# A tile of its own for each PSUM bank of the Strassen chains, and another order for the first two column groups

## Chip, cores and metric

The kernel runs on one core of a Trainium2 chip. The metric is the device time of one execution in microseconds, the median of several runs. Engines are called by the profile's names: PE is TensorE (PEld its weight loads), DVE VectorE, ACT ScalarE, POOL GpSimd, SP the DMA queue of SyncE.

## What is computed

A linear attention with decay (batch 2, 8 heads, 768 steps, head size 64) gives x with 1536 tokens of 512 features. A first mixture of experts sends each token to one of 8 experts. A second one runs all tokens through 4 experts:

```python
p = domain_probs / (domain_probs.sum(-1, keepdims=True) + 1e-09)
for e in range(E):                       # E = 4, w1[e]: 512 x 1024, w2[e]: 1024 x 512
    h = np.maximum(x @ w1[e], 0.0)
    out += p[:, e:e + 1] * (h @ w2[e])
```

The change concerns this second mixture. In the profile it runs from 240.75 us to the end.

## The kernel before

Everything is float32, written as a high and a low part (`float32r`): a value is cast on ACT to its high part, and DVE subtracts that from the value to get the low part. A product of two such operands is three matmuls (high by high, high by low, low by high; `PASS`). The order of the work is written out by hand: each engine executes its instructions in the order in which the program names them, and waits are put in where tiles ask for it.

The second mixture works in 32 **column groups** n. Group n belongs to a half s of the tokens (768 each), an expert e and a quarter q of the 1024 hidden columns. Its first layer multiplies the half's features, a 2 x 2 arrangement of blocks (256 features x 384 tokens each), with a 2 x 2 arrangement of weight blocks, by seven products instead of eight (Strassen). `front(n)` (line 972) issues the seven: `product(n, i, bank, first)` is six matmuls of 384 columns, two halves of the 256 features by three passes. The token operands `X1` to `X7` are blocks of x or sums of blocks (`x_sum`, `x_hi`, `x_lo`, lines 750 to 773), made once for each half of the tokens; the weight operands are the loaded blocks `p` or sums of them `t` (`combine_w`, line 134, three instructions), each split into two parts (`split_w`, line 116).

The products gather in two PSUM banks, a and b. Bank a takes products 1, 6, 7 and 4, one on top of the other; b takes 2, and then, newly begun, 5 and 3. Between them ACT copies the state of a to a `c` tile (`kept`, line 963) and DVE adds b to it (`joined`, line 968), so the four results c11, c22, c12 and c21 come out (c21 straight from a). Each result goes through ReLU on ACT (its high part) and one DVE instruction (its low part), `evac_h`, line 955; the pair is a tile `g` of 384 tokens.

`back(n, t)` (line 1050) is the second layer of a group for the 128 tokens of tile t, t = 0 to 5: six matmuls of 512 columns into an output bank o, which gathers over the four quarters q of an expert. Behind the fourth, `leave` (line 1091) lets DVE scale the bank by the token's weight and add it to the sum in SBUF; in the last expert `send` stores it from POOL.

The main loop interleaves front(n) with the six steps of the group before: products 1, 2, step 0, product 6, step 1, products 5, 7, steps 2, 3, products 3, 4, steps 4, 5. The splits of the next weights stand in between, and `combine_w(n + 2)` on POOL at the end. `load_w` issues the weight loads of 512 KB on SP, four of them in flight.

PSUM has eight banks. The pool `ps1` gives them out as four tiles of two banks, and `twin` (line 937) hands these on: a and b are the two halves of one tile (`ab`), and the output banks of steps 0 and 1, 2 and 3, 4 and 5 share a tile each:

```python
def front(n):
    ab = twin(0, f"ab{n}")
    a, b = ab[:, 0], ab[:, 1]
...
    bk = gb[t // 2][:, t % 2]
```

The first two groups have no group before them to be interleaved with. `first_pair` (line 998) runs products of both in turn: 1, 7, 2, 6, 5, 4, 3. There products 7 and 4 have a third tile `dd`, so DVE adds dd to c12 for c22 and for c21. Meanwhile the X tiles are made; x_sum(0,3), combine_w(2) and combine_w(3) run on POOL. Six output steps of group 0 follow.

Of the kernel before, what the change touches and what calls it, by code (L numbers as in the profile page):

```python
# [54 lines left out]
def tile_retention_moe_moe(ctx: ExitStack, tc, qkv, cst, gqt, a1, a2, b1, b2, out, cap):  # L55
# [674 lines left out]
    offsets()  # L730
    xe[2] = load_xe(2)
    sctx.close()
    ps[0] = ctx.enter_context(tc.tile_pool(name="ps1", bufs=1, space=PSUM))
    nduo = [0]

    def duo(name):
# [123 lines left out]
    for e in range(E1):  # L860
# [92 lines left out]
    hq = {}  # L953

    def evac_h(n, c, src):
        h2 = hq[n, c] = ph.tile([P, 2, HT], F32R, tag="h", name=f"g{n}_{c}")
        nc.scalar.activation(out=h2[:, 0], in_=src, func=AF.Relu)  # L957
        nc.vector.scalar_tensor_tensor(  # L958
            out=h2[:, 1], in0=src, scalar=0.0, in1=h2[:, 0].bitcast(F32), op0=ALU.max,
            op1=ALU.subtract,  # L960
        )

    def kept(n, c, bk):
# [6 lines left out]
        evac_h(n, c, t)  # L970

    def front(n):
        ab = twin(0, f"ab{n}")
        a, b = ab[:, 0], ab[:, 1]
        product(n, 1, a, True)
        c11 = kept(n, "c11", a)
        yield
        product(n, 2, b, True)
        joined(n, "c11", b, c11)
        yield  # L980
        product(n, 6, a, False)
# [12 lines left out]
        evac_h(n, "c21", a[:, 0:HT])
        del ws["p", n], ws["t", n]
        yield

    def first_pair():
        add = ALU.add
        ab = [twin(n, f"ab{n}") for n in range(2)]  # L1000
        dd = twin(2, "dd")
        c11, c12, c22 = [0, 0], [0, 0], [0, 0]

        def each(i, bank, first):
            for n in range(2):
                product(n, i, dd[:, n] if bank == 2 else ab[n][:, bank], first)

        each(1, 0, True)
        c11[0] = kept(0, "c11", ab[0][:, 0])
# [12 lines left out]
        each(2, 1, True)
        x_hi(0, 4)
        for n in range(2):
            joined(n, "c11", ab[n][:, 1], c11[n])
        x_lo(0, 4)
        each(6, 0, False)
        x_hi(0, 3)
        x_lo(0, 3)
        for n in range(2):  # L1030
            c12[n] = kept(n, "c12", ab[n][:, 0])
            c22[n] = pk.tile([P, HT], F32, tag="c22", name=f"c22_{n}")
            nc.vector.tensor_tensor(out=c22[n], in0=dd[:, n, 0:HT], in1=c12[n], op=add)
        each(5, 1, True)
        for n in range(2):
            joined(n, "c22", ab[n][:, 1], c22[n])
        each(4, 2, False)
        split_w(units.index(("w", 0)))
        for n in range(2):
            c21 = pk.tile([P, HT], F32, tag="c11", name=f"c21_{n}")  # L1040
            nc.vector.tensor_tensor(out=c21, in0=dd[:, n, 0:HT], in1=c12[n], op=add)
            evac_h(n, "c21", c21)
        each(3, 1, False)
        for n in range(2):
            joined(n, "c12", ab[n][:, 1], c12[n])
            del ws["p", n], ws["t", n]

    gb = {}

    def back(n, t):  # L1050
        s, e, q = n // 16, n // 4 % E2, n % 4
        if q == 0 and t // 2 not in gb:
            gb[t // 2] = twin(3 - t // 2, f"o{n}_{t}")
        bk = gb[t // 2][:, t % 2]
        hs = [hq[n, c] for c in (("c11", "c12") if t < 3 else ("c21", "c22"))]
        cols = slice(t % 3 * P, t % 3 * P + P)
        w = ws["w", n].rearrange("p s (k d) -> p s k d", k=2)
        for k in range(2):
            for m, (sh, sw) in enumerate(PASS):
                nc.tensor.matmul(  # L1060
                    out=bk, lhsT=hs[k][:, sh, cols], rhs=w[:, sw, k],
                    start=(q == 0 and k == 0 and m == 0), stop=(k == 1 and m == 2),
                    skip_group_check=True,
                )
        if q == 3:
            leave(s, e, t, bk)
            if t % 2:
                del gb[t // 2]
            if s and e == E2 - 1:
                send(s, t)  # L1070

# [188 lines left out]
```

## Time and profile before

| | us |
|---|---|
| median of three runs | 874.26 (872.3 to 874.83) |
| profiled execution | 876.1 |
| its span, from the first to the last instruction | 874.0 |
| PE busy | 770.9 (88% of the span) |
| DVE busy | 487.0 (56%) |
| ACT busy | 339.8 (39%) |
| POOL busy | 173.8 (20%) |
| PE busy from 75 to 235 (first mixture) | 159.19 of 160 |
| PE busy from 338 to 556 (second mixture) | 191.13 of 218 |

The profile follows one execution. Where an engine was idle in front of an instruction, the row names in brackets for how long and what released it ("0.62 <-ACT c L965": for 0.62 us, until ACT's instruction that writes tile c in line 965 was done). A matmul's end is modelled; the rate of a row of matmuls is read from the start of one row to the start of the next. The granted clock of PE is given as a share of 2.4 GHz; it has two levels here, 1.00 and 0.50.

### The profile page before, as it was taken

What the parts mean: (1) busy time and instruction counts of PE and PEld (TensorE: products, weight loads), DVE (VectorE), ACT (ScalarE), POOL (GpSimd) and SP (SyncE); (2) the same over time, 40 slices, a digit from 0 to 9 for tenths busy, and PEclk for the clock granted to TensorE, in tenths of its full rate; (3) what the DMA queues carried; (4) which work ended last, traced back from release to release, by engine and by line L of the source; (5) the groups of instructions that cost most, each with busy time, mean ns of one, the idle gap of its engine ahead of it and who ended that gap; (6) DMA issues with size and microseconds to landing.
All of it is one profiled execution on the core that took longest, in us unless ns stands there. A gap on an engine that the chain in (4) does not pass through costs nothing.

```text
span 874.0 us, 11369 instructions
## 1 busy us (share of the span) xinstructions
PE 770.9 (88%) x4466; PEld 670.6 (77%) x4467; DVE 487.0 (56%) x773; ACT 339.8 (39%) x550; POOL 173.8 (20%) x165
## 2 busy tenths in 40 slices
PE   8989999999988988997998897799979979988993
PEld 6878999999976867876877776678867767877772
DVE  4888788788884453445445537543544444454431
ACT  2345666666543332332433334233423323432320
POOL 3532111321041120111111113151112111111002
PEclk9999999999998998999999998999999999999998
DMA  9966677666402211121121121022211121121001
GB/s 343 410 231 231 229 232 233 219 202 212 145 25 73 72 49 49 49 73 49 49 72 49 49 72 47 27 100 81 71 43 67 51 70 49 49 72 49 1 1 72
DMA packets 27642, 93.22 MB, mean 107 GB/s; under 512 B 3617, under 2 KB 3889, under 8 KB 27586
## 3 DMA queue, kind: packets, MB, share of 16 engines
q1 hardware_dynamic: 23042, 81.79, 27.8%
q0 software_dynamic: 2672, 7.44, 2.4%
q10 hardware_dynamic: 1872, 3.24, 1.0%
q8 instruction: 36, 0.59, 0.3%
q14 instruction: 20, 0.16, 0.1%
HBM read 86.11 MB, written 6.34 MB: 106 GB/s over the span
## 4 chain that ended last, share of the span: by engine, by line
PE 76%; DVE 13%; ACT 6%; issue 2%; DMA 1%; POOL 1%; ACTq 0%; POOLq 0%; SPq 0%; DVEq 0%
PE o L1060 28%; PE ab L948 26%; PE m L852 12%; PE m L855 6%; DVE w L127 4%; DVE c L969 3%; ACT c L965 2%; ACT w L126 2%; DVE X L772 1%; DVE x L1106 1%; ACT g_c L957 1%; DVE g_c L958 1%; PE S L248 1%; PE X L346 1%; PE O L303 1%
## 5 line engine op out<-in xcount | busy, mean ns | idle before, releaser
L1060 PE MATMUL o<-w,g_c 128*128 128x512 f32 x1152 | 299.3, 404 | 33.2 <-DVE x L1106 19.3
L948 PE MATMUL ab<-X,w 128*128 128x384 f32 x1320 | 274.2, 348 | 46.2 <-DVE c L969 27.3
L948 PEld LDWEIGHTS ab<-X,w 128*128 128x128 f32 x1320 | 237.0, 192 | 77.3 <-DVE c L969 35.2
L1060 PEld LDWEIGHTS o<-w,g_c 128*128 128x128 f32 x1152 | 218.1, 193 | 83.4 <-DVE x L1106 26.6
L127 DVE TENSOR_TENSOR w<-raw,w 128x1024 fp32r<-128x1024 f32 x128 | 157.0, 1230 | 76.7 <-ACT w L126 76.1
L126 ACT CAST w<-raw 128x1024 fp32r<-128x1024 f32 x128 | 133.4, 1048 | 1.3 <-ACT xk L365 1.2
L969 DVE TENSOR_TENSOR c<-ab,c 128x384 f32<-128x384 f32 x96 | 53.4, 556 | 140.2 <-PE ab L948 133.3
L957 ACT ACTIVATE g_c<-c 128x384 fp32r<-128x384 f32 x98 | 51.5, 525 | 198.7 <-DVE c L969 195.8
L141 POOL TENSOR_TENSOR t<-raw 128x512 f32<-128x512 f32 x30 | 39.7, 1324 | 386.2 <-DMA raw<-b 294.9
L965 ACT COPY c<-ab 128x384 f32<-128x384 f32 x94 | 45.0, 479 | 174.4 <-PE ab L948 174.4
L958 DVE SCALAR_TENSOR_TENSOR g_c<-c,g_c 128x384 fp32r<-128x384 f32 x98 | 60.9, 621 | 59.7 <-ACT g_c L957 59.7
L852 PE MATMUL m<-h,w 128*128 128x448 f32 x256 | 81.4, 377 | 0.8 <-DVE h L881 0.8
L852 PE MATMUL m<-xet,w 128*128 128x448 f32 x256 | 80.8, 375 | 1.5 <-DVE offb L549 1.5
L855 PE MATMUL m<-h,w 128*128 128x224 f32 x256 | 67.4, 263 | 0.0
L855 PE MATMUL m<-xet,w 128*128 128x224 f32 x256 | 67.4, 263 | 0.0
L852 PEld LDWEIGHTS m<-xet,w 128*128 128x128 f32 x256 | 48.0, 187 | 5.3 <-issue 1.6
L852 PEld LDWEIGHTS m<-h,w 128*128 128x128 f32 x256 | 48.0, 188 | 4.7 <-ACT w L126 1.1
L855 PEld LDWEIGHTS m<-h,w 128*128 128x128 f32 x256 | 48.8, 191 | 0.0
L855 PEld LDWEIGHTS m<-xet,w 128*128 128x128 f32 x256 | 48.8, 190 | 0.0
L1106 DVE SCALAR_TENSOR_TENSOR x<-o,tl,x 128x512 f32<-128x512 f32 x34 | 25.4, 747 | 26.1 <-PE o L1060 26.1
L127 DVE TENSOR_TENSOR w<-t,w 128x1024 fp32r<-128x1024 f32 x32 | 39.5, 1235 | 0.0
L126 ACT CAST w<-t 128x1024 fp32r<-128x1024 f32 x32 | 33.6, 1050 | 0.0
(137 smaller groups left out, 557.8 us busy)
## 6 DMA issues: line engine op xcount, KB each, us to landing
raw<-a SPq DMA_DIRECT2D x64, 512.0 KB, 4.3
raw<-b SPq DMA_DIRECT2D x64, 512.0 KB, 3.4
qk<-qkv SPq DMA_DIRECT2D x12, 512.0 KB, 7.6
kv<-qkv SPq DMA_DIRECT2D x12, 512.0 KB, 9.0
xd<-xk ACTq DMA_DIRECT2D x12, 256.0 KB, 6.4
gqs<-gqt SPq DMA_DIRECT2D x6, 256.0 KB, 7.4
iw<-cst SPq DMA_DIRECT2D x1, 272.0 KB
xe<-xd,gidx POOLq DMA_INDIRECT x16, 5.7
```

The lines of the kernel that those rows point to most:

```text
L126: nc.scalar.copy(w[:, 0], r)
L127: nc.vector.tensor_tensor(out=w[:, 1], in0=r, in1=w[:, 0].bitcast(F32), op=ALU.subtract)
L141: eng.tensor_tensor(out=c[:, 0:2], in0=b[:, 2:4], in1=b[:, 1:3], op=sub)
L852: nc.tensor.matmul(out=b2, lhsT=w[0], rhs=x, start=first, stop=last, skip_group_check=True)
L855: nc.tensor.matmul(out=b2[:, 0], lhsT=w[1], rhs=x[:, 0], start=False, stop=last, skip_group_check=True)
L948: nc.tensor.matmul(out=bk[:, 0:HT], lhsT=w[:, sw, k], rhs=x[:, sx, k], start=(first and m == 0), stop=(m == len(steps) - 1), skip_group_ch ...
L957: nc.scalar.activation(out=h2[:, 0], in_=src, func=AF.Relu)
L958: nc.vector.scalar_tensor_tensor(out=h2[:, 1], in0=src, scalar=0.0, in1=h2[:, 0].bitcast(F32), op0=ALU.max, op1=ALU.subtract,)
L965: nc.scalar.copy(t, bk[:, 0:HT])
L969: nc.vector.tensor_tensor(out=t, in0=bk[:, 0:HT], in1=t, op=ALU.add)
L1060: nc.tensor.matmul(out=bk, lhsT=hs[k][:, sh, cols], rhs=w[:, sw, k], start=(q == 0 and k == 0 and m == 0), stop=(k == 1 and m == 2), skip_ ...
L1106: nc.vector.scalar_tensor_tensor(out=to, in0=src, scalar=sc, in1=acc, op0=ALU.mult, op1=ALU.add)
```

## The change

Four things are changed.

The pool `ps1` is closed before the second mixture, and a new one, `ps2`, gives out eight tiles of one bank each (`pbank`). a and b are tiles of their own, b is a new tile when product 5 begins it again (`bb`), and each output step t has its own bank (`OB`).

`first_pair` runs the products in the order 1, 2, 5, 6, 7, 3, 4 for both groups, a and b as in `front`, with a third bank (`bb`) for 5 and 3. The tile dd is gone, and with it DVE's four sums of dd and c12.

x_sum(0,3) and combine_w(2) move from POOL to DVE, combine_w(2) to the end of `first_pair`. The sums of the two groups (`join`) stand together on DVE, ahead of the two low parts; `evac_h` is cut into its ACT half and its DVE half for that, and the g tiles are taken in the order of the groups.

Four pools get `reuse_waits="tile"`: a tile that takes the place of a closed pool's tile waits for that tile, not for the whole pool.

The diff, cut to its core:

```diff
-    ps[0] = ctx.enter_context(tc.tile_pool(name="ps1", bufs=1, space=PSUM))
+    pctx = ExitStack()
+    ps[0] = pctx.enter_context(tc.tile_pool(name="ps1", bufs=1, space=PSUM))
...
     hctx.close()
-    ph = ctx.enter_context(tc.tile_pool(name="ph2", bufs=8, side="right"))
-    pk = ctx.enter_context(tc.tile_pool(name="pk", bufs=2, side="right"))
+    pctx.close()
+    ph = ctx.enter_context(tc.tile_pool(name="ph2", bufs=8, side="right", reuse_waits="tile"))
+    pk = ctx.enter_context(tc.tile_pool(name="pk", bufs=2, side="right", reuse_waits="tile"))
+    ps2 = ctx.enter_context(tc.tile_pool(name="ps2", bufs=1, space=PSUM, reuse_waits="tile"))
...
-    def twin(k, name):
-        return ps[0].tile([P, 2, 512], F32, tag=f"duo{k}", name=name)
+    def pbank(k, name):
+        return ps2.tile([P, 512], F32, tag=f"k{k}", name=name)
...
     def front(n):
-        ab = twin(0, f"ab{n}")
-        a, b = ab[:, 0], ab[:, 1]
+        a, b = pbank(0, f"a{n}"), pbank(1, f"b{n}")
...
+        b = pbank(1, f"bb{n}")
         product(n, 5, b, True)
...
     def first_pair():
...
-        each(7, 2, True)
-        x_hi(0, 5)
-        x_lo(0, 5)
-        x_hi(0, 6)
-        x_lo(0, 6)
-        x_sum(0, 3, nc.gpsimd)
-        combine_w(2, nc.gpsimd)
-        each(2, 1, True)
...
+        each(2, b, True)
+        x_sum(0, 6, nc.vector)
+        x_hi(0, 5)
+        x_lo(0, 5)
+        each(5, bb, True)
+        x_hi(0, 6)
+        x_lo(0, 6)
+        each(6, a, False)
+        join("c11", b)
+        x_sum(0, 3, nc.vector)
...
+        each(7, a, False)
+        x_hi(0, 4)
+        x_lo(0, 4)
+        for n in two:
+            c[n, "c22"] = kept(n, "c22", a[n])
+        join("c22", bb)
+        each(3, bb, False)
...
+        each(4, a, False)
+        join("c12", bb)
...
+        combine_w(2, nc.vector)
...
     def back(n, t):
-        if q == 0 and t // 2 not in gb:
-            gb[t // 2] = twin(3 - t // 2, f"o{n}_{t}")
-        bk = gb[t // 2][:, t % 2]
+        if q == 0 and t not in gb:
+            gb[t] = pbank(OB[t], f"o{n}_{t}")
+        bk = gb[t]
```

PE in the main loop: product 4 of group 4, steps 4 and 5 of group 3 (the last quarter of an expert), products 1 and 2 of group 5. `ab` is the tile of two banks, `o0_4` the tile of steps 4 and 5, w78 a weight tile, g3 the results of group 3. Before:

```order
L948 MATMUL ab4_3675<-X0_4_3284,w76_3596 128x384 [waits DVE_49]
L948 MATMUL ab4_3675<-X0_4_3284,w76_3596 128x384 x5
L1060 MATMUL o0_4_3392<-w77_3654,g3_c21_3651 128x512 x3
L1060 MATMUL o0_4_3392<-w77_3654,g3_c22_3620 128x512 x3
L1060 MATMUL o0_4_3392<-w77_3654,g3_c21_3651 128x512 [waits DVE_49]
L1060 MATMUL o0_4_3392<-w77_3654,g3_c21_3651 128x512 x2
L1060 MATMUL o0_4_3392<-w77_3654,g3_c22_3620 128x512 x3
L948 MATMUL ab5_3798<-X0_1_3169,w78_3709 128x384 x6
L948 MATMUL ab5_3798<-X0_2_3243,w78_3709 128x384 [waits Activation_49]
```

The same place in the changed kernel, where a4, a5, b5, o0_4 and o0_5 are tiles of one bank:

```order
L951 MATMUL a4_3685<-X0_4_3334,w76_3605 128x384 [waits Activation_49]
L951 MATMUL a4_3685<-X0_4_3334,w76_3605 128x384 x5
L1091 MATMUL o0_4_3242<-w77_3664,g3_c21_3661 128x512 x3
L1091 MATMUL o0_4_3242<-w77_3664,g3_c22_3630 128x512 x3
L1091 MATMUL o0_5_3410<-w77_3664,g3_c21_3661 128x512 x3
L1091 MATMUL o0_5_3410<-w77_3664,g3_c22_3630 128x512 x3
L951 MATMUL a5_3810<-X0_1_3169,w78_3720 128x384 [waits DVE_49]
L951 MATMUL a5_3810<-X0_1_3169,w78_3720 128x384 x5
L951 MATMUL b5_3811<-X0_2_3260,w78_3720 128x384 x6
```

The matmuls and their order are the same. Product 4 waits for ACT instead of DVE, step 5 and product 2 wait for nothing, product 1 waits for DVE.

DVE in the first pair, from the first sum for c11 to the first sum for c22 out of b; c11_0 is the tile of group 0, X0_3 and X0_4 are splits of X tiles, x2 is x. Before:

```order
L969 TENSOR_TENSOR c11_0_3240<-ab0_3225,c11_0_3240 128x384
L958 SCALAR_TENSOR_TENSOR g0_c11_3287<-c11_0_3240,g0_c11_3287 128x384
L969 TENSOR_TENSOR c11_1_3245<-ab1_3226,c11_1_3245 128x384
L958 SCALAR_TENSOR_TENSOR g1_c11_3291<-c11_1_3245,g1_c11_3291 128x384
L772 TENSOR_TENSOR X0_4_3284<-x2_1152,X0_4_3284 128x768
L772 TENSOR_TENSOR X0_3_3307<-x2_1152,X0_3_3307 128x768
L1033 TENSOR_TENSOR c22_0_3312<-dd_3227,c12_0_3310 128x384
L1033 TENSOR_TENSOR c22_1_3316<-dd_3227,c12_1_3314 128x384
L969 TENSOR_TENSOR c22_0_3312<-ab0_3225,c22_0_3312 128x384
```

And in the changed kernel:

```order
L1031 TENSOR_TENSOR c11_0_3258<-ab0_1_3238,c11_0_3258 128x384
L1031 TENSOR_TENSOR c11_1_3262<-ab1_1_3240,c11_1_3262 128x384
L762 TENSOR_TENSOR x2_1152<-x2_1152 128x2x384
L971 SCALAR_TENSOR_TENSOR g0_c11_3229<-c11_0_3258,g0_c11_3229 128x384
L971 SCALAR_TENSOR_TENSOR g1_c11_3233<-c11_1_3262,g1_c11_3233 128x384
L773 TENSOR_TENSOR X0_3_3319<-x2_1152,X0_3_3319 128x768
L773 TENSOR_TENSOR X0_4_3334<-x2_1152,X0_4_3334 128x768
L1031 TENSOR_TENSOR c22_0_3337<-bb0_3243,c22_0_3337 128x384
```

The two sums for c11 stand together, x_sum(0,3) (line 762) has come in behind them, and the sums of dd are gone.

## Rows read from the trace of the kernel before

**Rows 1.** Waits of the whole run: engine, line, releaser: us, times, longest.
```profile
PE ab L948 <- DVE c L969: 27.3, 32, 5.8
PE o L1060 <- DVE x L1106: 19.3, 12, 2.0
PE ab L948 <- ACT c L965: 18.9, 30, 0.9
```

**Rows 2.** Timeline of PE in one group: start, us, instruction, count, idle before.
```profile
360.10 2.25 PE L948 MATMUL ab<-X,w 128*128 128x384 f32 x12
362.19 2.92 PE L1060 MATMUL o<-w,g_c 128*128 128x512 f32 x12
364.95 1.23 PE L948 MATMUL ab<-X,w 128*128 128x384 f32 x6
366.82 1.33 PE L948 MATMUL ab<-X,w 128*128 128x384 f32 x6 [0.65 <-DVE c L969]
...
370.75 1.22 PE L948 MATMUL ab<-X,w 128*128 128x384 f32 x6
372.60 1.33 PE L948 MATMUL ab<-X,w 128*128 128x384 f32 x6 [0.62 <-ACT c L965]
```

**Rows 3.** Timeline of ACT, then DVE, in the same stretch.
```profile
368.19 0.49 ACT L957 ACTIVATE g_c<-ab 128x384 fp32r<-128x384 f32 x1 [0.81 <-PE ab L948]
...
372.07 0.48 ACT L965 COPY c<-ab 128x384 f32<-128x384 f32 x1 [2.45 <-PE ab L948]
...
360.42 1.23 DVE L127 TENSOR_TENSOR w<-raw,w 128x1024 fp32r<-128x1024 f32 x1 [2.17 <-ACT w L126]
...
366.21 0.56 DVE L969 TENSOR_TENSOR c<-ab,c 128x384 f32<-128x384 f32 x1 [1.60 <-PE ab L948]
367.42 1.10 DVE L958 SCALAR_TENSOR_TENSOR g_c<-c,g_c 128x384 fp32r<-128x384 f32 x1 [0.65 <-ACT g_c L957]
```

**Rows 4.** Timeline of PE where an expert's last quarter leaves.
```profile
400.74 1.66 PE L1060 MATMUL o<-w,g_c 128*128 128x512 f32 x6 [1.65 <-DVE x L1106]
...
408.89 1.67 PE L1060 MATMUL o<-w,g_c 128*128 128x512 f32 x6 [2.05 <-DVE x L1106]
```

**Rows 5.** Timeline of PE in the first pair, up to group 2.
```profile
240.75 2.25 PE L948 MATMUL ab<-X,w 128*128 128x384 f32 x12
...
249.59 1.28 PE L948 MATMUL ab<-X,w 128*128 128x384 f32 x6 [2.42 <-DVE c L969]
...
266.90 9.26 PE L1060 MATMUL o<-w,g_c 128*128 128x512 f32 x30 [1.07 <-DVE c L969]
275.99 1.22 PE L948 MATMUL ab<-X,w 128*128 128x384 f32 x6
```

**Rows 6.** Timeline of DVE, then POOL, at the end of the kernel.
```profile
850.48 0.75 DVE L1106 SCALAR_TENSOR_TENSOR x<-o,tl,x 128x512 f32<-128x512 f32 x1 [1.51 <-PE o L1060]
...
851.51 0.99 POOL L1073 DMA_INDIRECT out_dram<-x,tl  x1 [62.37 <-DVE x L1106]
854.98 0.97 POOL L1073 DMA_INDIRECT out_dram<-x,tl  x1 [2.47 <-DMA out_dram<-x,tl]
```

**Rows 7.** Timeline of PE, then DVE, in group 15.
```profile
531.61 1.29 PE L948 MATMUL ab<-X,w 128*128 128x384 f32 x6
538.73 2.29 PE L948 MATMUL ab<-X,w 128*128 128x384 f32 x6 [5.82 <-DVE c L969]
...
538.13 0.54 DVE L969 TENSOR_TENSOR c<-ab,c 128x384 f32<-128x384 f32 x1
```

**Rows 8.** Timeline of ACT, then DVE, in the first pair.
```profile
242.91 0.84 ACT L768 CAST X<-x 128x768 fp32r<-128x768 f32 x1 [0.42 <-DVE x L915]
...
243.78 0.95 DVE L772 TENSOR_TENSOR X<-x,X 128x768 fp32r<-128x768 f32 x1
...
245.53 3.45 DVE L772 TENSOR_TENSOR X<-x,X 128x768 fp32r<-128x768 f32 x2
```

**Rows 9.** Busy us (instructions) of each engine in a stretch, PEclk, DMA share, GB/s.
```profile
75.00:235.00 160.00, 159.19 (x1033) 151.87 (x1032) 132.45 (x179) 102.41 (x153) 30.65 (x26) 1.00 0.68 221
```

More of the change, by code (lines that the diff above doesn't have):

```diff
@@ L899, in tile_retention_moe_moe @@
             mctx.close()
-            px2 = ctx.enter_context(tc.tile_pool(name="px2", bufs=1))
+            px2 = ctx.enter_context(tc.tile_pool(name="px2", bufs=1, reuse_waits="tile"))
         for d in range(KD):
@@ L953, in tile_retention_moe_moe, with h_tile, evac_hi, evac_lo @@
     hq = {}
-    def evac_h(n, c, src):
-        h2 = hq[n, c] = ph.tile([P, 2, HT], F32R, tag="h", name=f"g{n}_{c}")
+    gb = {}
+    OB = (7, 2, 3, 4, 5, 6)
+    def h_tile(n, c):
+        hq[n, c] = ph.tile([P, 2, HT], F32R, tag="h", name=f"g{n}_{c}")
+    def evac_hi(n, c, src):
+        if (n, c) not in hq:
+            h_tile(n, c)
+        h2 = hq[n, c]
         nc.scalar.activation(out=h2[:, 0], in_=src, func=AF.Relu)
+    def evac_lo(n, c, src):
+        h2 = hq[n, c]
         nc.vector.scalar_tensor_tensor(
@@ L961, in evac_h @@
         )
+    def evac_h(n, c, src):
+        evac_hi(n, c, src)
+        evac_lo(n, c, src)
     def kept(n, c, bk):
@@ L998, in first_pair @@
     def first_pair():
[L999 to L1009, printed above, removed]
+        two = range(2)
+        for n in two:
+            for k in ("c11", "c22", "c12", "c21"):
+                h_tile(n, k)
@@ new lines, in first_pair, with each, join @@
+        ab = [[pbank(2 * n + j, f"ab{n}_{j}") for j in two] for n in two]
+        gb.update({t: pbank(OB[t], f"o0_{t}") for t in (3, 4)})
+        bb = [pbank(6 + n, f"bb{n}") for n in two]
+        c = {}
+        def each(i, bks, first):
+            for n in two:
+                product(n, i, bks[n], first)
+        def join(k, bks):
+            for n in two:
+                nc.vector.tensor_tensor(
+                    out=c[n, k], in0=bks[n][:, 0:HT], in1=c[n, k], op=ALU.add
+                )
@@ L1010, in first_pair @@
+        a, b = [x[0] for x in ab], [x[1] for x in ab]
+        each(1, a, True)
         x_sum(0, 5, nc.vector)
+        c[0, "c11"] = kept(0, "c11", a[0])
         x_hi(0, 2)
-        c11[1] = kept(1, "c11", ab[1][:, 0])
+        c[1, "c11"] = kept(1, "c11", a[1])
         x_lo(0, 2)
+        each(2, b, True)
         x_sum(0, 6, nc.vector)
-        each(7, 2, True)
         x_hi(0, 5)
         x_lo(0, 5)
+        each(5, bb, True)
         x_hi(0, 6)
         x_lo(0, 6)
-        x_sum(0, 3, nc.gpsimd)
@@ L1021, in first_pair @@
-        combine_w(2, nc.gpsimd)
-        each(2, 1, True)
[L1023 to L1027, printed above, removed]
+        each(6, a, False)
+        join("c11", b)
+        x_sum(0, 3, nc.vector)
+        for n in two:
+            evac_hi(n, "c11", c[n, "c11"])
+        for n in two:
+            c[n, "c12"] = kept(n, "c12", a[n])
+            evac_lo(n, "c11", c[n, "c11"])
         x_hi(0, 3)
         x_lo(0, 3)
[L1030 to L1037, printed above, removed]
-        split_w(units.index(("w", 0)))
[L1039 to L1045, printed above, removed]
+        each(7, a, False)
@@ new lines, in first_pair @@
+        x_hi(0, 4)
+        x_lo(0, 4)
+        for n in two:
+            c[n, "c22"] = kept(n, "c22", a[n])
+        join("c22", bb)
+        each(3, bb, False)
+        for n in two:
+            evac_hi(n, "c22", c[n, "c22"])
+        for n in two:
+            evac_lo(n, "c22", c[n, "c22"])
+        split_w(units.index(("w", 0)))
+        each(4, a, False)
+        join("c12", bb)
+        for n in two:
+            evac_hi(n, "c21", a[n][:, 0:HT])
+            evac_hi(n, "c12", c[n, "c12"])
+            evac_lo(n, "c21", a[n][:, 0:HT])
+            evac_lo(n, "c12", c[n, "c12"])
@@ L1046, in first_pair @@
             del ws["p", n], ws["t", n]
-    gb = {}
+        combine_w(2, nc.vector)
     def back(n, t):
         s, e, q = n // 16, n // 4 % E2, n % 4
-        if q == 0 and t // 2 not in gb:
-            gb[t // 2] = twin(3 - t // 2, f"o{n}_{t}")
-        bk = gb[t // 2][:, t % 2]
+        if q == 0 and t not in gb:
+            gb[t] = pbank(OB[t], f"o{n}_{t}")
+        bk = gb[t]
         hs = [hq[n, c] for c in (("c11", "c12") if t < 3 else ("c21", "c22"))]
@@ L1065, in back @@
         if q == 3:
-            leave(s, e, t, bk)
-            if t % 2:
-                del gb[t // 2]
+            leave(s, e, t, gb.pop(t))
             if s and e == E2 - 1:
```

## The prediction

> **What bounds the kernel now.** I began with the list of waits over the whole run. TensorE is the busiest engine, and below its name three lines stand out [rows 1]: products waiting for VectorE's sums (27.3 us in 32 waits), products waiting for ScalarE's copies (18.9 us in 30), output matmuls waiting for VectorE's outgoing sums (19.3 us in 12). The counts matter more than the sums: 30 is the number of column groups from n = 2 to 31, so each of the first two waits comes once per group. Write P1 to P7 for the products of a group and b0 to b5 for its output steps.
>
> Then the timeline of one group [rows 2]. Without a wait, 12 matmuls of 384 columns take 362.19 - 360.10 = 2.09 us (1.04 a product) and 12 of 512 columns 364.95 - 362.19 = 2.76 us (1.38 a step). P3 starts at 364.95 and is through at 365.99, but P4 starts only at 366.82, named releaser VectorE's sum c. P1 starts at 370.75 and is through at 371.79, P2 starts at 372.60, named releaser ScalarE's copy c. Neither wait is for data. P4 writes the half a of the tile ab while the sum reads the half b; P2 writes b while the copy reads a. The times fit to the hundredth: the sum starts at 366.21 and lasts 0.56, the copy at 372.07 and lasts 0.48 [rows 3]. So per group 0.83 + 0.81 us are lost.
>
> Every fourth group b3 waits for the outgoing sum of b2 and b5 for that of b4, 1.65 and 2.05 us [rows 4], again two halves of one tile. The first pair of groups has true gaps (2.42 us before 249.59, 1.07 before 266.90) and, after them, the lower of TensorE's two clock levels: 30 matmuls of 512 columns take 9.26 us where 30 x 0.23 would be 6.9 [rows 5]. That is 2.4 us lost to 1.2 GHz.
>
> **The loop, n = 2 to 31.** The order of the built program shows that the four kinds of wait are gone from TensorE: P2, b1, b3, b5 wait for nobody, P4 waits for its own bank's copy alone. A group is then 7 x 1.04 + 6 x 1.38 = 15.58 us, if nothing true is late. So I lay VectorE's and ScalarE's queues along it, from P1 at 0: P2 1.04, b0 2.08, P6 3.47, b1 4.51, P5 5.90, P7 6.94, b2 and b3 7.98, P3 10.74, P4 11.78, b4 and b5 12.82, next P1 15.58. A copy starts 1.32 us after its product's start (370.75 to 372.07), a sum 1.26 us after (364.95 to 366.21) [rows 2, 3].
> - P6 needs the copy of P1: 1.32 + 0.48 = 1.80, wanted at 3.47.
> - P7 needs the copy of P6: 3.47 + 1.80 = 5.27, wanted at 6.94.
> - P3 needs the sum c22 out of its bank. The copy of P7 ends at 8.74; the two weight splits ahead on VectorE (1.23 each [rows 3], the first 1.77 ahead of b2 as at 360.42, so at 6.2) end at 8.6; the sum ends at 9.34, wanted at 10.74.
> - P1 of the next group needs the low part of c21 out of bank a. The sum c12 runs from 12.00 to 12.56, ScalarE's two activations end at 13.6 (0.5 each), VectorE's two low parts at 14.3, or 14.8 if one takes the 1.10 us of 367.42 [rows 3]. Wanted at 15.58.
> The least margin is 0.8 us. In a group with outgoing sums two of them (0.75 us each [rows 6]) stand before the sum c12 and put the last low part at 14.4 to 15.0: margin 0.6. The last two run into the next group, ahead of its first sum at 17.9, and end by 17.5. So TensorE stays the bound: 30 x 15.58 = 467.4 us. The weight loads follow the splits, which move with the groups, and are used more than a group later, so DMA costs nothing.
>
> The Trainium skill (SBUF — State Buffer, Who interferes with whom) says that a VectorE instruction with two SBUF inputs contends with a GpSimd instruction that reads SBUF. By that rule the low part of c12 takes the 1.10 us in every group that meets combine_w there, and the margin is 0.8, not 1.3: the sum stays, the first rival's chance goes up.
>
> **The exception, n = 15.** There the token half changes, and VectorE's queue has the splits of new X tiles ahead of the sum c12. P3 starts at 531.61, the sum only at 538.13, P4 at 538.73 after 5.82 us of idle [rows 7]. In the changed kernel P4, b4, b5 don't wait. Everything runs 0.9 earlier (P2's gap and the slow start behind it are gone): P3 at 530.7, b5 through at 530.7 + 2 x 1.04 + 2.76 = 535.5. P1 of n = 16 needs the low part of c21: sum at 537.2, + 0.54, two activations and a low part to 539.5. So 4.0 us of stall remain, and behind it the lower clock (P4's 2.29 us for six matmuls in that row), taken at the 2.4 us above. 6.4 us; between 4.0 and 8 without and with a longer stretch at 1.2 GHz.
>
> **The first pair.** VectorE loses the four sums that read dd (lines 1033 and 1041, about the 0.55 of another sum) and takes x_sum(0,3) and combine_w(2) from GpSimd; the rest is order. P1 of both groups runs from 240.75 to 242.83 as before. The new second step, P2, needs X2: its high part is on ScalarE from 242.91 to 243.75, its low part on VectorE from 243.78 to 244.73 [rows 8]. So a new stall of 1.0 us, where P7 filled the gap; P2 ends at 246.2. P5 and P6 need the low parts of X5 and X6. Before, these two took 3.45 us beside GpSimd, against 0.95 for one alone [rows 8]. combine_w(3) stays on GpSimd, and its buffers are free by 245, so I keep the slow value: X5 low at 247.8, X6 low at 249.2. P5 ends at 249.1, P6 at 251.2, P7 at 253.3. P3 waits for the sum c22, which stands on VectorE behind two sums c11 (0.55 each), x_sum(0,3) (0.95, as large as the split at 243.78), two low parts, and the splits X3 and X4 (0.95 each): it ends at 255.0. A stall of 1.75 us. P3 and P4 end at 259.2; 36 output matmuls x 0.23 = 8.3 and 0.3 for the last low part give 267.8 for P1 of n = 2, which was at 275.99 [rows 5]. combine_w(2), now on VectorE behind the last low parts at 261, costs about the 1.23 us of a split of as many columns; the splits of n = 2 that need it are done by 265, 2.8 us before they are used. Bounds: 266 if GpSimd doesn't overlap; 270.2 if a stall brings 1.2 GHz on for as long as behind 266.90. I take 267.8, the longest stall being shorter than the 2.42 us before 249.59.
>
> **The end.** Six stores on GpSimd, each waiting for the one before (851.51, 854.98, ...), close the kernel; the first needs only b0 of n = 31 and its outgoing sum (850.48, 0.75) [rows 6]. From 851.51 to 874.0 is 22.5 us, and none of it moves: b1 to b5 of the last group lose their waits for nothing.
>
> **The sum.** 267.8 + 467.4 + 6.4 = 741.6; b0 of n = 31 with 0.1 for its weights 1.5: 743.1; 0.2 + 0.75 + 0.3 to the first store: 744.3; + 22.5 = 766.8 us of span. The profiled execution was 2.1 longer than its span (876.1) and 1.8 over the median: 767 us for the median.
>
> **Rivals.**
> 1. A true wait takes the place. The thinnest margin is P1 behind the low part of c21 (0.6 to 0.8 us). Were VectorE or ScalarE 1.1 to 1.9 us later there than I reckon, each group would lose 0.5 to 1.1: 30 x that is 15 to 33, so 782 to 800. For it: the 1.10 us row. Against: it is in the margin already. 12%.
> 2. Own banks buy nothing: what is named as releaser is not what TensorE waits for. Then only the first pair moves, 8.2 us: 866. Against: the gaps end 0.05 us after the named copy and sum. The Trainium skill (TensorE: Matmul & The Clock Gate, HAM oscillation) tells of a kernel in which more PSUM buffers brought no further gain. By that rule this rival holds; here the waits are on the reader of the other half, so it gets 2%.
> 3. Slower: the denser loop doesn't keep 2.4 GHz. If a share h of the loop ran at 1.2 GHz it would take 467 x (1 + h). Before, 575.5 us lie between P1 of n = 2 and the first store, after 476.5, and the first pair gives 8.2: the kernel is slower than before from h = (575.5 + 8.2 - 476.5) / 467 = 0.23; at 0.26 it is 889. For it: the lower level does occur [rows 5]. Against: in 160 us of the first layers TensorE was busy for 159.19 at a granted clock of 1.00 [rows 9]; the lower level came only behind gaps. 3%.
>
> **How the numbers follow.** The forecast has 83%. Its own range is 763 (first pair 266, no lower clock at n = 15) to 774 (270.2, 8 us at n = 15, a tenth of a microsecond lost per group). The range of 761 to 783 adds the light end of the first rival and leaves out about 16%. A measurement of this kernel can tell about 0.3% from no change. Faster by over that are the forecast and rivals 1 and 2: 0.97. The third rival gives 0.01 to within it, near its point of decision, and 0.02 to slower.
>
> **What would show it.** In the changed profile: no idle time before P2 and P4; a group every 15.6 us, those with outgoing sums too; granted clock 1.00 except behind n = 15; one stall of about 4 us there; P1 of n = 2 near 268; 22.5 us from the first store to the end. A stall in front of P1 in every group would be the first rival. The prediction fails if another pair of engines meets at a bank in each group, or if VectorE falls behind by over 0.6 us.

## The result and the profile after

| | before | after |
|---|---|---|
| median of runs, us | 874.55 (872.3 to 876.11, 4 runs) | 769.48 (769.13 to 770.58, 4 runs) |
| profiled execution, us | 876.1 | 769.24 |
| its span, us | 874.0 | 767.5 |
| PE busy | 770.9 (88%) | 734.6 (96%) |
| first product of the first pair to the first store, us | 610.76 | 504.25 |

The ratio is 0.8802, with a 95% interval of 0.8781 to 0.8824: 12.0% less time. The forecast was 767 us, in a range of 761 to 783.

Waits of PE over the whole run of the changed kernel (engine, line, releaser: us, times, longest), the answer to [rows 1]:

```profile
PE a L951 <- DVE g_c L971: 3.7, 1, 3.7
...
PE bb L951 <- DVE c L1031: 1.5, 1, 1.5
```

The three repeated waits (27.3, 19.3 and 18.9 us) are gone. What is left in the second mixture came once each: 3.7 us at group 15, and 1.5, 0.8 and 0.5 us in the first pair. The list of before also held 7.5 us in 4 waits for outgoing sums of line 1104 and 2.0 us in one of the tile `last`, which [rows 1] leave out; they are gone too.

Timeline of PE in one group, with an expert's outgoing sums in it (start, us, instruction, count); it answers [rows 2] and [rows 4]:

```profile
361.29 1.23 PE L951 MATMUL a<-X,w 128*128 128x384 f32 x6
362.36 1.20 PE L951 MATMUL b<-X,w 128*128 128x384 f32 x6
...
372.06 1.23 PE L951 MATMUL bb<-X,w 128*128 128x384 f32 x6
373.13 1.20 PE L951 MATMUL a<-X,w 128*128 128x384 f32 x6
374.17 2.92 PE L1091 MATMUL o<-w,g_c 128*128 128x512 f32 x12
376.93 1.23 PE L951 MATMUL a<-X,w 128*128 128x384 f32 x6
```

P2 (tile b, 362.36) stands 1.07 us behind P1, P4 (373.13) 1.07 behind P3, b4 and b5 are one row without idle time, and no row carries a bracket. From one P1 to the next it is 376.93 - 361.29 = 15.64 us.

DVE: the low parts of c12 and c21 in the group before; then, in the stretch of PE above, the sum c12, its low part, and the low part of c21, which must be through before the next P1 (376.93 above):

```profile
358.90 0.56 DVE L971 SCALAR_TENSOR_TENSOR g_c<-c,g_c 128x384 fp32r<-128x384 f32 x1 [0.65 <-ACT g_c L967]
359.37 0.55 DVE L971 SCALAR_TENSOR_TENSOR g_c<-a,g_c 128x384 fp32r<-128x384 f32 x1
...
373.42 0.55 DVE L986 TENSOR_TENSOR c<-bb,c 128x384 f32<-128x384 f32 x1
374.62 1.13 DVE L971 SCALAR_TENSOR_TENSOR g_c<-c,g_c 128x384 fp32r<-128x384 f32 x1 [0.65 <-ACT g_c L967]
375.67 0.55 DVE L971 SCALAR_TENSOR_TENSOR g_c<-a,g_c 128x384 fp32r<-128x384 f32 x1
```

The low part of c21 is through at 376.22, 0.71 us before P1. In the group before, without outgoing sums, it ends at 359.92 (359.37 + 0.55) and P1 starts at 361.29: 1.37 us. What makes the difference is less the outgoing sums than the low part of c12, 1.13 us here and 0.56 there: of the groups n = 2 to 30 without 15, nine have a low part of c12 of 0.89 to 1.14 us and margins of 0.71 to 0.91, four of them without outgoing sums; where it takes 0.56 the margin is 1.37 to 1.43, or 0.97 in group 16 with outgoing sums. This margin is what the runs with one and four VectorE instructions more measure.

The first pair, PE and then DVE with the two slow low parts and the later ones of X3 and X4; the answer to [rows 5] and [rows 8]:

```profile
240.72 2.26 PE L951 MATMUL ab<-X,w 128*128 128x384 f32 x12
243.76 2.68 PE L951 MATMUL ab<-X,w 128*128 128x384 f32 x12 [0.78 <-ACT X L769]
...
247.60 1.67 PE L951 MATMUL bb<-X,w 128*128 128x384 f32 x8 [0.46 <-DVE X L773]
...
254.97 2.35 PE L951 MATMUL bb<-X,w 128*128 128x384 f32 x12 [1.55 <-DVE c L1031]
...
259.24 8.37 PE L1091 MATMUL o<-w,g_c 128*128 128x512 f32 x36
267.45 1.23 PE L951 MATMUL a<-X,w 128*128 128x384 f32 x6
...
245.49 3.45 DVE L773 TENSOR_TENSOR X<-x,X 128x768 fp32r<-128x768 f32 x2
...
252.63 1.83 DVE L773 TENSOR_TENSOR X<-x,X 128x768 fp32r<-128x768 f32 x2 [0.94 <-ACT X L769]
```

P1 of n = 2 starts at 267.45, against 275.99 before. The 36 output matmuls take 267.45 - 259.24 = 8.21 us, 0.228 each, the full clock, where 30 of them took 9.26 before.

Group 15, PE: P4, steps b4 and b5, and P1 of n = 16 behind its stall; then DVE, from two low parts of X to the low part of c21. The answer to [rows 7]:

```profile
482.68 1.20 PE L951 MATMUL a<-X,w 128*128 128x384 f32 x6
483.72 2.92 PE L1091 MATMUL o<-w,g_c 128*128 128x512 f32 x12
490.38 2.29 PE L951 MATMUL a<-X,w 128*128 128x384 f32 x6 [3.75 <-DVE g_c L971]
...
483.33 3.46 DVE L773 TENSOR_TENSOR X<-x,X 128x768 fp32r<-128x768 f32 x2
486.71 1.47 DVE L773 TENSOR_TENSOR X<-s,X 128x768 fp32r<-128x768 f32 x1
488.11 0.54 DVE L986 TENSOR_TENSOR c<-bb,c 128x384 f32<-128x384 f32 x1
...
489.78 0.55 DVE L971 SCALAR_TENSOR_TENSOR g_c<-a,g_c 128x384 fp32r<-128x384 f32 x1
```

P4 no longer stalls; P1 of n = 16 does, until the low part of c21 is through at 490.33. Three low parts of X (483.33 to 488.18) stand ahead of the sum c12.

Stretches of the loop, with the stall in the middle one (busy us of PE, PEld, DVE, ACT and POOL with their instructions, PEclk, DMA share, GB/s), to be read against [rows 9]:

```profile
267.45:486.00 218.55, 218.55 (x1091) 196.84 (x1090) 120.08 (x158) 89.12 (x142) 48.86 (x45) 1.00 0.21 68
486.00:496.00 10.00, 6.25 (x24) 5.54 (x23) 7.64 (x10) 4.31 (x7) 1.32 (x1) 0.83 0.15 52
496.00:742.00 246.00, 246.00 (x1228) 221.59 (x1227) 132.85 (x181) 96.82 (x156) 49.16 (x48) 1.00 0.19 65
```

PE is busy for every hundredth of the first and the third stretch, at a granted clock of 1.00, that is 2.4 GHz.

### The profile page after: what moved, and what is told of

Same layout as the page of the kernel before. It is cut to its first block, busy times and chain, and to the rows that moved or that the text cites. A ratio compares the mean times of both kernels' runs of the same rounds, so it can differ in the third digit from the quotient of the medians.

```text
span 767.5 us, 11364 instructions
## 1 busy us (share of the span) xinstructions
PE 734.6 (96%) x4466; PEld 664.9 (87%) x4467; DVE 480.9 (63%) x773; ACT 337.1 (44%) x552; POOL 172.8 (23%) x161
## 4 chain that ended last, share of the span: by engine, by line
PE 85%; DMA 6%; DVE 5%; ACT 1%; issue 1%; POOL 0%; POOLq 0%; ACTq 0%; SPq 0%; DVEq 0%
PE o L1091 34%; PE a L951 16%; PE m L853 13%; PE bb L951 8%; PE m L856 6%; PE b L951 4%; DMA raw<-a 2%; DMA kv<-qkv 2%; DVE X L773 1%; DMA out_dram<-x,tl 1%; DVE w L127 1%; DMA xd<-xk 1%; PE T L703 1%; PE ab L951 1%; ACT w L126 1%
## 5 line engine op out<-in xcount | busy, mean ns | idle before, releaser
L1091 PE MATMUL o<-w,g_c 128*128 128x512 f32 x1152 | 285.0, 392 | 0.0
L1091 PEld LDWEIGHTS o<-w,g_c 128*128 128x128 f32 x1152 | 214.3, 188 | 39.3 <-DVE w L127 0.2
L951 PE MATMUL a<-X,w 128*128 128x384 f32 x720 | 146.1, 337 | 3.7 <-DVE g_c L971 3.7
L951 PEld LDWEIGHTS a<-X,w 128*128 128x128 f32 x720 | 128.9, 189 | 9.1 <-DVE g_c L971 4.2
L982 ACT COPY c<-a 128x384 f32<-128x384 f32 x90 | 43.3, 481 | 142.5 <-PE a L951 142.5
L951 PE MATMUL bb<-X,w 128*128 128x384 f32 x384 | 77.9, 338 | 2.0 <-DVE c L1031 1.5
L951 PEld LDWEIGHTS bb<-X,w 128*128 128x128 f32 x384 | 68.7, 188 | 7.8 <-DVE c L1031 1.9
L986 DVE TENSOR_TENSOR c<-bb,c 128x384 f32<-128x384 f32 x60 | 33.3, 555 | 41.8 <-PE bb L951 34.8
L986 DVE TENSOR_TENSOR c<-b,c 128x384 f32<-128x384 f32 x30 | 16.7, 557 | 55.6 <-PE b L951 55.6
```

Source lines behind the costliest of these rows:

```text
L951: nc.tensor.matmul(out=bk[:, 0:HT], lhsT=w[:, sw, k], rhs=x[:, sx, k], start=(first and m == 0), stop=(m == len(steps) - 1), skip_group_ch ...
L986: nc.vector.tensor_tensor(out=t, in0=bk[:, 0:HT], in1=t, op=ALU.add)
L1091: nc.tensor.matmul(out=bk, lhsT=hs[k][:, sh, cols], rhs=w[:, sw, k], start=(q == 0 and k == 0 and m == 0), stop=(k == 1 and m == 2), skip_ ...
```

## The experiments

The programs came in three groups, each beside runs of the kernel before: the first four below (before: 874.22 us), the next four (874.75), the last two (869.62). Executions of one changed program differ by 1 to 4 us, and in the profiles the first pair starts anywhere from 239.07 to 240.80. So effects below 0.5% are read from the profiled executions: the time from the first product of the first pair to the first store, called **the section** here (after: 744.97 - 240.72 = 504.25 us).

### Each half of the cut alone, and both

In each of these three runs the old PSUM pool is also closed behind the first pair and a new one opened with `reuse_waits="tile"`, which the diffs leave out.

**Own banks for a and b alone**, on the kernel before:

```diff
     def front(n):
-        ab = twin(0, f"ab{n}")
-        a, b = ab[:, 0], ab[:, 1]
+        a, b = [ps[0].tile([P, 512], F32, tag=f"k{j}", name=f"{'ab'[j]}{n}") for j in range(2)]
...
+        b = ps[0].tile([P, 512], F32, tag="k1", name=f"bb{n}")
         product(n, 5, b, True)
```

> The kernel before with one part of the change alone: in the main loop the product banks a and b are tiles of their own; the first pair and the output banks in pairs stay. False-wait theory: P2 and P4 wait for nobody, 59 gaps of 0.82 us and 0.13 for each restart, 59 x 0.95 = 56 us less, but the waits of b3 and b5 in 7 groups stay, and may grow to 2.3 us each since VectorE is asked for earlier: 815 to 826 us, most likely 821, a group without outgoing sums every 15.6 us. Own banks buy nothing (rival 2): 874 us, with the 0.8 us gaps still there under another releaser.

Measured: 819.07 us (815.81 to 819.2), ratio 0.9374 (0.9316 to 0.9433). Waits of PE in this kernel:

```profile
PE o L1061 <- DVE x L1107: 19.8, 12, 2.3
...
PE a L949 <- DVE g_c L959: 3.7, 1, 3.7
```

Its timeline of PE where an expert's last quarter leaves (P1, P2 and b3):

```profile
376.28 1.23 PE L949 MATMUL a<-X,w 128*128 128x384 f32 x6
377.34 1.20 PE L949 MATMUL b<-X,w 128*128 128x384 f32 x6
...
387.89 1.66 PE L1061 MATMUL o<-w,g_c 128*128 128x512 f32 x6 [1.67 <-DVE x L1107]
```

The gap before P2 is gone (1.06 us from P1), the wait of b3 is there. 874.22 - 819.07 = 55.2 us, against the 56 expected, or 53 with the growth of the other waits (821). The waits for the outgoing sums hardly grew: 19.8 us in 12, where it was 19.3.

**Own banks for the output steps alone**, on the kernel before:

```diff
-        if q == 0 and t // 2 not in gb:
-            gb[t // 2] = twin(3 - t // 2, f"o{n}_{t}")
-        bk = gb[t // 2][:, t % 2]
+        if q == 0 and t not in gb:
+            gb[t] = obank(n, t)
+        bk = gb[t]
```

> The kernel before with the other half of the loop's change alone: each output step has its own bank; a and b still share a tile. False-wait theory: b1, b3 and b5 of 7 groups lose their waits for the outgoing sums, about 4.7 us per such group or 33 us, and some of the time at the lower clock behind them, about 8 us: 830 to 838 us, most likely 834; the 0.8 us gaps before P2 and P4 stay in each group. Rival 2: 874 us.

Measured: 834.36 us (833.65 to 834.51), ratio 0.956 (0.9502 to 0.9618). Its waits of PE:

```profile
PE ab L949 <- DVE c L970: 28.2, 32, 5.8
PE ab L949 <- ACT c L966: 18.9, 30, 0.9
```

The outgoing sums have left the list, and the gaps before P2 and P4 are as long as before. 39.9 us saved, 40 expected. The waits for outgoing sums on the list of before, those of line 1104 and of `last` with them, are 28.8 us; behind them was time at the lower clock, too: from 275 to 480 us the granted clock was 0.98 before and is 1.00 here, from 555 to 740 us 0.97 and 1.00.

**Both, with the first pair of before** (the two diffs together):

> The kernel before's first pair with all banks of the loop as tiles of their own. If what the loop saves and what the first pair saves are independent, this is the changed kernel plus the 8.5 us by which its P1 of n = 2 comes earlier (275.99 against 267.45): 776 to 780 us, most likely 778. Rival 2 (own banks buy nothing, the new first pair is all): 874 us. A third reading, that the new first pair is what keeps the loop dense: over 785 us.

Measured: 777.81 us (774.38 to 778.79), ratio 0.8916 (0.8862 to 0.897). The halves gave 55.2 + 39.9 = 95.0 apart and 96.4 together, so within the spread of the runs they are independent. This rules the second rival out: the same eight banks, with the same matmuls in the same order, give 96 us once no two of them share a tile. The first pair is worth the rest, 777.81 - 769.48 = 8.3 us, of which the profile of this kernel shows only 6.4, since there the output matmuls behind the stall ran at the full clock (this execution took 774.38 us at a mean granted clock of 0.989, the other four 777.35 to 778.79 at 0.980 to 0.983):

```profile
265.26 7.10 PE L1064 MATMUL o<-w,g_c 128*128 128x512 f32 x30 [1.51 <-DVE c L970]
272.20 1.23 PE L949 MATMUL a<-X,w 128*128 128x384 f32 x6
```

With its first product at 239.09, P1 of n = 2 comes 33.11 us after it; before it was 35.24 (275.99 - 240.75), in the changed kernel 26.73. The 2.1 us between the first two are the lower clock of [rows 5], which came in that execution and not in this one.

### The four pool settings

```diff
-    ps2 = ctx.enter_context(tc.tile_pool(name="ps2", bufs=1, space=PSUM, reuse_waits="tile"))
+    ps2 = ctx.enter_context(tc.tile_pool(name="ps2", bufs=1, space=PSUM))
```

and the same for the pools of the X tiles, the g tiles and the c tiles.

> The changed kernel without the four settings by which a tile waits for the tile it replaces and not for the closed pool. In the built order the first splits and copies of the first pair then wait for the whole pool, up to the sum of two blocks of x at 242.84. Theory: 1 to 2.2 us later at P1 of n = 2, the loop as in the changed kernel, 770.5 to 771.7 us. Rival: the wait is hidden, since the first products wait for x anyway: 769.5 us.

Measured: 771.2 us (769.79 to 772.54). PE's P1 and P2 of the first pair, and P1 of n = 2; then a stretch of the first row, in the columns of [rows 9]:

```profile
242.90 6.01 PE L951 MATMUL ab<-X,w 128*128 128x384 f32 x24 [2.01 <-DVE x L916]
...
269.60 1.23 PE L951 MATMUL a<-X,w 128*128 128x384 f32 x6
...
243.90:247.00 3.10, 3.10 (x12) 3.10 (x11) 1.16 (x2) 1.69 (x4) 2.16 (x2) 0.50 0.01 4
```

The first product waits for the sum of line 916 (2.01 us) and starts 2.18 us later than in the changed kernel. Behind that wait the granted clock is 0.50 from 243.90 to 247.00, so P1 and P2 take 5.85 us (242.90 to 248.75) where 24 such matmuls at the full clock take 4.18 (2 x 2.09), and no wait shows before P2 or P5. P1 of n = 2 is 2.15 us later than there. I had said nothing of these settings in the sum. They are worth some 2 us, a quarter of what the first pair brings, but only beside the new pools: the first product of the kernel before started at 240.75 without them [rows 5]. Which of the four does it was not tried.

### GpSimd beside the low parts of X5 and X6

```diff
-            combine_w(3, nc.gpsimd)
+            combine_w(3, nc.vector)
```

> The changed kernel with combine_w(3), which runs on GpSimd beside the low parts of X5 and X6, on VectorE behind the six output steps of the first pair. If GpSimd's reads of SBUF slow these low parts, they take 0.95 us each instead of 1.7, and P1 of n = 2 comes about 0.6 us earlier: 768.9 us. Rival: their slowness has another cause (the row covers a wait between the two): 3.45 us for the two as before, 769.5 us. Slower if the three sums on VectorE push the splits of n = 2 behind their use: over 770 us.

Measured: 769.22 us (767.02 to 769.67), by the medians not to be told from the changed kernel; the section is 743.01 - 239.53 = 503.48 us, 0.77 less. DVE's low parts of X5 and X6 and those of X3 and X4, and P3 and, 25.93 us after the pair's first product (26.73 in the changed kernel), P1 of n = 2:

```profile
244.30 1.94 DVE L773 TENSOR_TENSOR X<-x,X 128x768 fp32r<-128x768 f32 x2
...
250.66 1.83 DVE L773 TENSOR_TENSOR X<-x,X 128x768 fp32r<-128x768 f32 x2 [1.69 <-ACT X L769]
...
253.01 2.35 PE L951 MATMUL bb<-X,w 128*128 128x384 f32 x12 [1.55 <-DVE c L1031]
...
265.46 1.23 PE L951 MATMUL a<-X,w 128*128 128x384 f32 x6
```

With GpSimd silent the pair takes 1.94 us instead of 3.45, so it was GpSimd. The three sums on GpSimd had been slowed as well: 2.05, 1.33 and 1.34 us there, against 1.28, 0.74 and 0.74 at 267.15, where VectorE was idle but for the last 0.25 us. What was won is P5's wait alone: VectorE reaches X3 and X4 sooner, only to wait 1.69 us for ScalarE's high parts there instead of 0.94, and P3's stall stays at 1.55 us.

### The stall at group 15

The low parts of X5 and X7 are taken out from in front of the sum c12:

```diff
         back(n - 1, 3)
-        if swap:
-            x_split(1, 5)
-            x_split(1, 7)
         next(f)
         next(f)
         split_w(units.index(("w", n)))
+        if swap:
+            x_split(1, 5)
+            x_split(1, 7)
```

> The changed kernel with the splits of X5 and X7 of the second half of the tokens moved behind the weight split and the two products' sums of group 15, so that the sum c12 and the low part of c21 come earlier on VectorE. Theory: the 3.75 us stall before P1 of n = 16 shrinks to about 1.3 us and TensorE's lower clock behind it is gone: 4.1 us less, 765.4 us. Rival: the stall only moves, to P5 and P7 of group 16, which read X5 and X7: 769.5 us or a little above.

Measured: 765.83 us (763.46 to 766.59); the section is 739.20 - 239.14 = 500.06 us, 4.19 less than after. P1 of n = 16 in this kernel:

```profile
486.16 1.31 PE L951 MATMUL a<-X,w 128*128 128x384 f32 x6 [1.09 <-DVE g_c L971]
```

The stall is 1.09 us, and six matmuls behind it take 1.31 us instead of 2.29. From this P1 to the next it is 15.72 us (501.88 - 486.16), an ordinary group, where the changed kernel took 17.32 (507.70 - 490.38). Nothing stalls later, so the stall was this queue and no more. What is left of it is X6's low part, which stands in front of the sum c12 still.

### How thick is the margin

One VectorE instruction more in each group, in front of the low part of c21, and then (with range(4)) four of them; both only add work whose result nobody reads:

```diff
-        evac_h(n, "c21", a[:, 0:HT])
+        evac_hi(n, "c21", a[:, 0:HT])
+        for j in range(1):
+            nc.vector.tensor_tensor(out=junk[:, 0:HT], in0=a[:, 0:HT], in1=junk[:, 0:HT], op=ALU.max)
+        evac_lo(n, "c21", a[:, 0:HT])
```

> The changed kernel with one VectorE instruction more per group (a maximum over bank a, 0.56 us, whose result nobody reads) in front of the low part of c21. The margin between the end of that low part and the next P1 is 1.37 us in groups without outgoing sums and about 0.75 in those with them. Both are larger than 0.56: no change, 769.5 us, but for about 0.5 us at group 15 where the margin is nil: 769.5 to 770.5. Rival: VectorE is already as late as TensorE can bear, every microsecond on it counts: 30 x 0.56 = 17 us more, 786 us.

Measured: 769.14 us (768.52 to 771.38). DVE in the group with outgoing sums of the profile after, and PE's P1 behind it:

```profile
375.68 0.55 DVE L1014 TENSOR_TENSOR tsum<-a,tsum 128x384 f32<-128x384 f32 x1
376.14 0.54 DVE L972 SCALAR_TENSOR_TENSOR g_c<-a,g_c 128x384 fp32r<-128x384 f32 x1
...
377.01 1.23 PE L952 MATMUL a<-X,w 128*128 128x384 f32 x6
```

30 x 0.55 us more on VectorE, and no stall in any group but n = 15: in the waits "PE a" is one entry of 4.23 us instead of 3.75. The thinnest margin left elsewhere is 0.30 us. The section grows by 1.2 us, of which 0.5 is that stall, 0.6 a longer stretch at the lower clock behind it, and 0.1 the end of the loop.

> The changed kernel with four such VectorE instructions more per group (about 1.9 to 2.2 us) in front of the low part of c21. That is past the margins of 1.37 and 0.75 us by about 0.5 in 22 groups and 1.2 in 7, and each stall costs 0.13 to restart: about 23 us more, 785 to 800 us, most likely 790, with a stall in front of P1 in every group. If the margin were spent otherwise (other instructions late first): over 800 us. If VectorE has slack elsewhere: 769.5 us.

Measured: 808.05 us (807.53 to 810.63), past the range that I had given. Waits of PE:

```profile
PE a L952 <- DVE g_c L972: 32.3, 29, 6.0
```

Timeline: DVE and then P1 on PE in an ordinary group, P1 in one with outgoing sums, and step b0 of the last group:

```profile
365.40 2.33 DVE L1014 TENSOR_TENSOR tsum<-a,tsum 128x384 f32<-128x384 f32 x4
...
368.25 1.34 PE L952 MATMUL a<-X,w 128*128 128x384 f32 x6 [0.77 <-DVE g_c L972]
...
385.51 1.34 PE L952 MATMUL a<-X,w 128*128 128x384 f32 x6 [1.35 <-DVE g_c L972]
...
780.78 8.23 PE L1095 MATMUL o<-w,g_c 128*128 128x512 f32 x35 [1.67 <-DVE w L127]
```

The mechanism is the expected one, and its sizes fit the margins: the four push the low part back by 2.25 us (365.40 to 367.65). 2.25 - 1.37 = 0.88, and an ordinary group is 16.66 us instead of 15.64 (368.25 - 351.59), 1.02 more with the restart. 2.25 - 0.71 = 1.54, and the group of the last P1 shown is 17.26 (385.51 - 368.25), 1.62 more. In the whole loop 19 groups are 1.01 us longer on average and eight 1.57: those eight are the ones in which the low part of c12 takes 0.83 to 1.11 us instead of 0.56 to 0.62, six with outgoing sums and two without. My number was too small for three reasons that the rows show: I took 1.9 us for the four; at n = 15 the stall grew to 6.01 us, with more of the lower clock behind it, so that groups 15 and 16 are 2.4 and 2.2 us longer; and the last weight split came 1.67 us late for b0 of n = 31, the end of the loop being 2.0 us longer. 19 x 1.01 + 8 x 1.57 + 2.4 + 2.2 + 2.0 = 38.4, and the section is 38.4 us longer.

### A version that beats both

The edits of the two sections on GpSimd and on group 15 together:

> The changed kernel with both edits: combine_w(3) of the first pair on VectorE, and the splits of X5 and X7 at group 15 behind the weight split. In the traces of the two edits apart, P1 of n = 2 came 0.8 us earlier after the pair's first product with the one, and the stall before P1 of n = 16 fell from 3.75 to 1.09 us with the full clock behind it with the other. If the two add up: 765.8 less 0.8, 765.0 us. Rival, that what the first pair gives is lost again later: 765.8 us.

Measured: 763.93 us (762.92 to 764.92), ratio to before 0.8775 (0.8741 to 0.8808). The section is 740.06 - 240.80 = 499.26 us, 4.99 less than after, and 0.77 + 4.19 = 4.96: the two add up. The median is 1.1 us below what was expected, which proves nothing: beside this run the kernel before took 869.62 us, 4.9 less than beside the changed kernel.

With the split of X6 moved behind the weight split as well:

```diff
-        if swap:
-            x_split(1, 6)
         back(n - 1, 3)
         next(f)
         next(f)
         split_w(units.index(("w", n)))
         if swap:
+            x_split(1, 6)
             x_split(1, 5)
             x_split(1, 7)
```

> As the run before it, and the split of X6 at group 15 is moved behind the weight split too. In the trace with X5 and X7 moved, the low part of X6 stood 2.04 us long on VectorE, beside GpSimd, right ahead of the sum c12. Without it there the sum c12 and the low part of c21 come about 1.9 us earlier, and the stall of 1.09 us before P1 of n = 16 goes: 1.2 us less than the run before it, 763.8 us. Rival: the three splits in a row push the sum c11 of group 16 behind its use by P5 (0.3 us of margin by my reckoning), or X6 behind P6, and the stall only moves there: 764.5 to 766 us.

Measured: 764.15 us (761.99 to 765.73), ratio 0.8781 (0.8746 to 0.8815); the section is 737.74 - 239.07 = 498.67 us, 0.6 less than the run before it, half of the 1.2 that was expected. PE at n = 16:

```profile
484.06 1.23 PE L951 MATMUL a<-X,w 128*128 128x384 f32 x6
...
495.43 1.31 PE L951 MATMUL bb<-X,w 128*128 128x384 f32 x6 [0.28 <-DVE c L986]
```

P1 starts without a wait, and group 15 is 1.22 us shorter than in the run before it (15.72 and 16.94), as expected. But P3 now waits 0.28 us for the sum c22, and group 16 takes 16.32 us (500.38 - 484.06), 0.57 more than there. The rival named the right kind of wait and the wrong product. By the medians the two versions can't be told apart. Both are below every run of the changed kernel (769.13 us and up), but they ran beside faster runs of before, the intervals of the ratios overlap with its 0.8781 to 0.8824, and by its ratio the run with X5 and X7 alone (0.8758) is not behind them. That they beat the changed kernel rests on the sections, 5.0 and 5.6 us shorter in one profiled execution each, with each part at the row that the edit moved.

## Why the prediction was right

**What is waited for.** That P2 and P4 wait only because two banks are halves of one tile was argued before; the three runs on the halves show it. The Trainium skill (PSUM — Partial Sum Buffer, PSUM bank collisions raise a hardware error) says that PSUM is to be guarded by bank and quadrant, and that by bank is the simple version. The kernel before guarded two banks at a time, and in these runs the wider guard cost 96 us. The kernel that I had weighed, in which more PSUM buffers brought no further gain (the Trainium skill, TensorE: Matmul & The Clock Gate, HAM oscillation), doesn't meet this case, since no bank was added: all eight were in use before.

**The loop.** 15.58 us a group (the sum along the group; the product as written gives 15.56) was 0.06 too small: P1 and P3, which follow output steps, take 1.07 us and not 1.04 (361.29 to 362.36). 30 x 0.06 = 1.8 us. The margin was reckoned at 0.6 with outgoing sums and at 0.8 to 1.3 without; it is 0.71 and 1.37 in the two groups shown, but split by the slow low part of c12 more than by the outgoing sums. That low part is slow in nine of the 29 groups n = 2 to 30, not in every group that meets combine_w. With one instruction more nothing stalled, with four every group did, so the wait of the first rival is real and lies 0.7 us of VectorE's time away.

**Group 15.** Forecast: 4.0 us of stall and 2.4 of lower clock. b5 is through at 483.72 + 2.76 = 486.48, P1 starts at 490.38: 3.9. Group 16 is 1.7 us over an ordinary one. So the clock's term was 0.7 too large.

**The first pair.** 267.8 forecast, 267.45 measured. The steps came out within 0.1 us: P2 is through at 246.28 (246.2 forecast), P5 at 249.10 (249.1, with the wait of 0.46 us for X5 in it), P3 starts at 254.97 (255.0), P4 is through at 259.24 (259.2). The slow low parts took the 3.45 us, and the 0.3 us for the last low part did not come: P1 follows the 36 output matmuls at once. The 1.75 before P3, 1.55 by the row, is in part luck. I had VectorE's queue alone on the way to the sum c22. In the row at 252.63 VectorE waits 0.94 us for ScalarE's high parts of X3 and X4, which no term of mine has, and its other steps behind X6 took 5.0 us where I had reckoned 5.8; the run with combine_w(3) on VectorE shows which of the two decides, since there VectorE is free sooner and P3's stall is 1.55 us again. That no lower clock came behind these stalls was a choice between two rows. It held, but its reason, that the longest stall is shorter than 2.42 us, is a weak one: in the run without the pool settings the lower clock came behind 2.01 us.

**The end.** 767.5 - 744.97 = 22.5 us from the first store, as said.

**The sum.** -0.35 in the first pair, +1.8 in the loop, -0.8 at n = 15: 0.65 us, and the span is 767.5 against 766.8. That it is so little is luck too, since the three have opposite signs. The larger part of the miss of 2.5 us is the last step, from the span to the median. I took the median to lie 1.8 us under the profiled execution, as it did before; in the changed kernel it lies 0.24 over it. The kernel before varies more: its 11 executions beside the first experiments took 866.46 us at a mean granted clock of 0.984 and up to 876.82 at 0.972, and the profiled one, with 0.974, was a long one. That offset belonged to an execution, not to the program.

**The third rival** fell with the stretches above: 1.00 over 464.55 us of the loop, on either side of the one stall.

## What to carry to other kernels

A wait that comes once per iteration and ends just behind an engine that reads something else is a sign that two things share one guard; the cure is the cut of the tile, and it costs nothing where the banks are in use anyway. After such a cut, the margin of the next true wait can be read from the profile (its releaser's end against the waiter's start) and held against what is planned for that engine. An offset between one profiled execution and the median is not carried from one program to the next.

## What the runs showed of the hardware

**Who is slowed when VectorE and GpSimd meet.** The low part of c12 on DVE (two SBUF inputs) is shown above in two groups of the changed kernel, at 358.90 and 374.62; this is the third sum of combine_w on POOL in the same two:

```profile
358.98 1.07 POOL L143 TENSOR_TENSOR t<-raw,t 128x256 f32<-128x256 f32 x1
...
374.59 0.74 POOL L143 TENSOR_TENSOR t<-raw,t 128x256 f32<-128x256 f32 x1
```

At 358.90 VectorE is first by 0.08 us: it takes 0.56 and GpSimd 1.07 instead of 0.74. At 374.59 GpSimd is first by 0.03: it takes 0.74 and VectorE, in the row at 374.62, 1.13 instead of 0.56. The Trainium skill (SBUF — State Buffer, Who interferes with whom) says that issue order, not the operation's shape, decides who blocks; these rows agree. I had counted the 1.10 us of [rows 3] as a cost of the place, and it is a cost of 0.1 us of timing: in the kernel with one instruction more, GpSimd's sum starts at 358.97 and the low part at 358.98, and that group has the slow one (1.15 us) too.

**The lower clock behind a stall.** Behind the stall at n = 15 the group took 17.32 us in the changed kernel and 17.89 behind 4.23 us of stall; behind 1.09 us it took 15.72. So the lower level cost 1.7 to 2.3 us or nothing. Behind the 2.01 us at the start of the first pair, in the run without the pool settings, it cost 1.67 (5.85 us for 4.18). In the first pair of before, 30 output matmuls behind a wait took 9.26 us in its own profile and 7.10 in that of the kernel with both cuts. What decides there was not tried.
